# Attention with a one-expert MoE: p's four chunks packed 171 columns apart, and the second of its PSUM banks also lent out as a third single bank

## The chip, the cores and the metric

The kernel runs on one core of a Trainium2 chip. The metric is the device time of one execution in microseconds (us), as the median of the runs of the same program; lower is better.

## What is computed

The reference has two parts. The first is attention with pooled keys: `kv` (4 batches, 384 x 32 positions, 128 channels) is averaged over 4 x 4 patches to 768 positions and multiplied by `w_sr`, and the result serves as both keys and values for 12288 queries per batch:

```
s = scale * (q @ k.transpose(0, 2, 1))
a = np.exp(s - s.max(-1, keepdims=True))
a /= a.sum(-1, keepdims=True) + 1e-09
x = (a @ v).reshape(B * S, D)            # 49152 tokens, 128 channels
```

The second is a mixture of eight experts with one expert per token, the one whose gate logit is largest:

```
logits = x @ w_gate
e = argmax(logits);  gate = softmax(logits)[e]
y = gate * (np.maximum(x @ w1[e], 0.0) @ w2[e])
```

## The kernel before

**The blocks.** The 49152 tokens are cut into 96 blocks of 512 tokens (`block`, 24 per batch; a block is four chunks of 128 tokens). For a block, TensorE (PE) makes the scores in three pairs of banks (`scores`, tile `s`), ScalarE (ACT) takes `exp` of a pair (`e`, L897), VectorE (DVE) forms 1 + s - e in bf16 (`r`, L899), and PE multiplies the four chunks of `r` by the values (`values`, L914): nine matmuls for a chunk, 145 or 136 columns each, into the PSUM tile `po`. ACT and DVE take `po` apart into a high and a low fp16 part (`xp`, L929 and L930) and a copy of the logits (`lg`, L932), and a DMA turns `xp` into `x`. The expert part of an earlier block follows: `hidden` makes three tiles of hidden units (`ph`, one bank each, of three, one and one matmuls of 512 columns), ACT drains them (`X` L956, `g` L963), GpSimd (POOL) splits the first (`g` L958, L960), `rows` collects 32 matmuls of 128 columns in one bank (`py`), DVE scales it by the gate (`y`, L983) and a DMA writes it. In the page and in the rows each bank tile other than `s` and `po` is called `b`.

**PSUM.** `PSUM = {"s": 2, "po": 1, "b": 2}` (L320): two pairs of banks for `s`, one tile of two banks for `po` (chunks 256 columns apart, two to a bank), and two single banks `b`. The single banks serve the three hidden tiles and `py` of every block, and all small results of the preparation.

**The preparation.** While the blocks of one batch run, `keys` pools the next batch's `kv` and makes its keys, and `expert` prepares the expert that most tokens of the batch will take: norms, an order of hidden units, gathers of `w1` and `w2` by one-hot matrices (`PU`), all through the single banks. Near its end `po_` (another tile than `po`: a single bank) takes the product `pown`; `constant` (L831 to L837, four DVE instructions) reads it with a scale (`ws`, ready with `uy`) and adds a row to `w2U`. The op is given out as one piece and waits for `pown`, `uy`, `w2Ug` and `w2x`; the single bank of `po_` is held until it is done. After each of the first three batches, `general_step` handles tokens that belong to another expert: DVE finds them, POOL gathers their queries by an indirect DMA (L1212), and PE turns the gathered queries (L1231, tile `pq`) before the rest.

**What sets the order.** Nothing is issued in the order of the code. Each piece of work is an `Op` with an engine, an estimated duration, a due time and the tiles it needs; `Plan.order` (L105) simulates five engines and the slots of all pools with those estimates and always takes the op that can start first, by due time where several could. `Plan.issue` then writes the ops out in the order of their planned starts. In that list an op that takes a tile of a pool for the first time gets the slot that comes free first (L170), and the slot is taken until the last op that uses the tile has ended. The semaphores are put in afterwards by the tile framework, from the program's order and from what each instruction reads and writes. PE, ACT, DVE, POOL and the DMA queue of SP each work through their own list strictly in order, so an instruction that waits holds up all behind it. From 20 to 110 us the planner also fills gaps of PE with matmuls on constants (`fill`).

Of the kernel before, what the change touches and what calls it, by code (L numbers as in the profile page):

```python
# [9 lines left out]
F32 = mybir.dt.float32  # L10
# [51 lines left out]

TOKENS = {"qr", "qs", "qh", "qp", "qTh", "qT", "s", "e", "r", "po", "xh", "xl", "lg", "x", "ph", "gf", "gh", "g", "py", "ys", "o"}
NUDGE = {}


class Buf:
    def __init__(self, pool, make):
        self.pool, self.make, self.slot, self.tile, self.left, self.end = pool, make, None, None, 0, 0.0


class Op:
# [3 lines left out]
class Plan:  # L76
# [30 lines left out]
    def order(self):  # L107
# [15 lines left out]
        while count:  # L123
            best = None
            for e, ops in cand.items():
                pick = None
                for o in ops:
                    start = max(free[e], o.ready)
                    if o.lock:
                        start = max(start, locked)  # L130
                    for b in o.bufs:
                        if b.slot is None:
                            start = max(start, min(slots[b.pool]))
                    if start == math.inf:
                        continue
                    key = (max(start, free[e] + 0.1), o.at, o.n)
                    if pick is None or key < pick[0]:
                        pick = key, start, o
                if pick and (best is None or pick[1] < best[0]):
                    best = pick[1], pick[2]  # L140
# [26 lines left out]
            for b in o.bufs:  # L167
                first = b.slot is None
                if first:
                    b.slot = min(range(len(slots[b.pool])), key=lambda i: (slots[b.pool][i], i))  # L170
                    slots[b.pool][b.slot] = math.inf
                o.slot_of.append((b, first))
                b.left -= 1
                b.end = max(b.end, land)
                if not b.left:
                    slots[b.pool][b.slot] = b.end + 0.1
# [17 lines left out]
def attention_moe(ctx: ExitStack, tc, q, kv, w_sr, w_gate, w1, w2, out):  # L194
# [117 lines left out]
    def bc(t, n):  # L312
# [7 lines left out]
    PSUM = {"s": 2, "po": 1, "b": 2}  # L320
    plan = Plan({**SBUF, **PSUM})
    op = plan.op

    def buf(pool, shape, dtype=F32):
        where = psum if pool in PSUM else sb
        return Buf(pool, lambda name: where.tile(shape, dtype, name=name))

    def bank():
        return buf("b", [P, 512])
# [172 lines left out]
    def expert(b, at):  # L502
# [329 lines left out]
        def constant():  # L832
            t, sc = ow.tile, ws.tile[so, 15:16]
            nc.vector.tensor_scalar(t[so, 0], po_.tile[so, :P], sc, None, op0=ALU.mult)
            nc.vector.scalar_tensor_tensor(t[so, 1], po_.tile[so, :P], sc, t[so, 0], op0=ALU.mult, op1=ALU.subtract)
            nc.vector.tensor_scalar(t[so, 2], t[so, 0], own[so, UH:UH + 1], None, op0=ALU.mult)
            nc.vector.scalar_tensor_tensor(w2U.tile[so, UH - 1], t[so, 1], own[so, UH + 1:UH + 2], t[so, 2], op0=ALU.mult,  # L837
                                           op1=ALU.add)

        op("DVE", 1.0, constant, at + 31, [("pown", b), ("uy", b), ("w2Ug", b), ("w2x", b)], [("w2U", b)], [po_, ow, ws, w2U])  # L840
        op("DVE", .1, lambda: nc.vector.memset(cn[:, 31:32], 0.0), at + 36,
           [("Tb", b), ("uy", b), ("first", b), ("rest", b)], [("con", b)])

# [8 lines left out]
    def block(t):  # L852
# [30 lines left out]
               T - 1.4 * LEN, [("qp", t)], [("qTh", t), ("qT", t)], [qp, qT], lands=2.0, moves=1.2)  # L883

        r = buf("r", [P, KT, BLK], BF16)
        po = buf("po", [P, CH, 2 * P])
        for s in range(KT // 2):
            ps, e = buf("s", [P, 2, BLK]), buf("e", [P, 2, BLK])
            at = T + s * LEN / 3
# [16 lines left out]
        for c in range(CH):  # L906
            def values(c=c):
                for kt in range(KT):
                    mm(po.tile[:, c, :XW], r.tile[:, kt, c * P:(c + 1) * P], v16.tile[:, kt, :XW], kt == 0, kt == KT - 1)
                    if kt == 0:  # L910
                        for i, j in ((0, 0), (1, 0), (0, 1)):
                            mm(po.tile[:, c, :P + E], own_q(c, i), M.tile[:, j], False, False)

            op("PE", .55, values, T + LEN * (1.8 + c / 8), [("r", t), ("qT", t), ("Mx", b), ("v16x", b)], [("po", t, c), ("po", t)],  # L914
               [po, qT, r, M, v16])
        last = ("po", t)
        if t % NB == 0:
            k["lg"], k["mo"] = buf("lg", [P, NB * CH, XW - C]), buf("mo", [P, 4, NB * CH])
        if i == 0:
# [6 lines left out]
        xl = lambda: x.tile[:, CH:].rearrange("p j n -> p (j n)")  # L926
        xc = lambda c, i: x.tile[:, i * CH + c]
        A = T + LEN * 2.05
        op("ACT", .59, lambda: nc.scalar.copy(xp.tile[:, 0], po.tile[:, :, :C]), A, [last], [("xh", t)], [po, xp])  # L929
        op("DVE", .69, lambda: nc.vector.tensor_tensor(xp.tile[:, 1], po.tile[:, :, :C], xp.tile[:, 0], op=ALU.subtract),  # L930
           A + .5, [("xh", t)], [("xl", t)], [po, xp])
        op("ACT", .23, lambda: nc.scalar.copy(lg.tile[:, bs], po.tile[:, :, C:XW]), A + .6, [last], [("lg", t)], [po, lg])  # L932
        op("SP", 1.24, lambda: nc.sync.dma_start_transpose(x.tile, xp.tile.rearrange("p a j c -> p (a j c)")), A + 1,
           [("xl", t)], [("x", t)], [xp, x], lands=2.0, moves=1.2)
        if t == GROUPS[g][-1]:
# [5 lines left out]
        for u in range(UH):  # L941
# [20 lines left out]
            else:  # L962
                op("ACT", .69, lambda u=u, ph=ph, zu=zu: nc.scalar.activation(  # L963
                    gg.tile[:, u], ph.tile, AF.Relu, bias=zu()), at + .5,
                   [("ph", t, u), ("zb", b)], [("g", t)], [ph, gg, k["zb"]])
        py, y = bank(), buf("y", [P, CH, C])

        def rows():
            Lt, w = k["L"].tile, k["w2U"].tile
# [418 lines left out]
```

## Time and profile before

| | before |
|---|---|
| median of 3 runs | 855.87 us (855.49 to 857.4) |
| the profiled execution | 854.62 us, of which 852.9 us are the span from the first to the last instruction |
| PE busy | 774.7 us, 91% of the span |
| DVE busy | 657.8 us, 77% |
| ACT busy | 599.2 us, 70% |
| POOL busy | 577.1 us, 68% |
| chain that ended last | PE 53%, DVE 15%, POOL 10%, DMA 8%, ACT 8%, issue 4% |

"Busy" counts a matmul to its modelled end, so that a busy PE need not be a PE at its peak; a single matmul is some 0.17 us longer than the distance at which the next follows it. The "chain" follows the work that ended last back to the start, at each step to what released it. In the view of waits, a row names the engine and tile that waited, what it waited for, and the total, the number and the longest of these waits.

### The profile page before, as it was taken

The page shows a single profiled execution, that of the slowest core. Times are in us where ns is not written, and L with a number is a line of the kernel's source. Part 1 is how long each engine was busy: PE and PEld are TensorE (multiplying, and loading weights), DVE is VectorE, ACT ScalarE, POOL GpSimd, SP SyncE. Part 2 cuts the span into 40 slices and gives each one's busy share as a digit, 9 for nine tenths or more (in the row PEclk, how much of TensorE's full clock was granted, in tenths as well). Part 3 has the DMA queues.
Part 4 walks back from the last instruction along what each step waited for, and adds up shares of the span by engine and source line. Part 5 has one row for each costly group of instructions (what it writes and reads, how often), then busy time and mean ns, then how long its engine had stood idle before and what let it go on. Part 6 is the DMA issues. An engine that isn't in the chain of part 4 may idle for free.

```text
span 852.9 us, 22180 instructions
## 1 busy us (share of the span) xinstructions
PE 774.7 (91%) x8701; PEld 611.1 (72%) x8701; DVE 657.8 (77%) x1209; ACT 599.2 (70%) x958; POOL 577.1 (68%) x784
## 2 busy tenths in 40 slices
PE   5998899998999778999999987989999989999995
PEld 5586587786878656777776765777877867787774
DVE  4688777879779885867868998667897888767683
ACT  1466877877777556777678765677778776778772
POOL 0475889855689858656558997845657766657463
PEclk9999999999999999999999999999999999999998
DMA  9475989876788997776469879668466989656542
GB/s 334 120 187 107 224 190 242 170 148 119 144 207 194 200 187 195 161 133 152 103 144 226 216 166 251 145 146 181 88 122 147 162 173 191 135 118 130 117 102 64
DMA packets 328283, 139.48 MB, mean 164 GB/s; under 512 B 214590, under 2 KB 320194, under 8 KB 328176
## 3 DMA queue, kind: packets, MB, share of 16 engines
q1 hardware_dynamic: 327696, 137.80, 72.4%
q8 instruction: 69, 1.13, 0.6%
q14 instruction: 38, 0.31, 0.1%
q0 software_dynamic: 192, 0.17, 0.1%
q10 hardware_dynamic: 288, 0.07, 0.0%
HBM read 59.12 MB, written 26.94 MB: 101 GB/s over the span
## 4 chain that ended last, share of the span: by engine, by line
PE 53%; DVE 15%; POOL 10%; DMA 8%; ACT 8%; issue 4%; SPq 1%; POOLq 0%; ACTq 0%; DVEq 0%
PE b L306 26%; PE po L306 16%; PE s L306 10%; DVE r L899 6%; DMA kv<-in_kv_dram 2%; ACT e L897 2%; POOL g L960 2%; POOL kv L396 2%; DMA qT<-qp 2%; DMA gp<-in_q_dram,gi 2%; POOL qp L880 1%; DVE xp L930 1%; ACT g L963 1%; DMA x<-xp 1%; POOL g L958 1%
## 5 line engine op out<-in xcount | busy, mean ns | idle before, releaser
L899 DVE SCALAR_TENSOR_TENSOR r<-s,e 128x1024 bf16<-128x1024 f32 x288 | 347.6, 1216 | 88.7 <-ACT e L897 87.1
L897 ACT ACTIVATE e<-s 128x1024 f32<-128x1024 f32 x288 | 294.3, 1030 | 92.8 <-PE s L306 87.8
L306 PE MATMUL po<-v,r 128*128 128x145 f16 x2304 | 254.3, 230 | 8.2 <-DVE xp L930 6.3
L306 PE MATMUL s<-qT,KT 128*128 128x512 f16 x576 | 168.7, 380 | 23.2 <-DVE r L899 20.9
L306 PEld LDWEIGHTS <-r 128*128 128x128 bf16 x2304 | 171.0, 100 | 25.2 <-issue 4.6
L306 PE MATMUL b<-w2U,g 128*128 128x128 f16 x1920 | 171.7, 220 | 3.4 <-POOL g L960 3.2
L963 ACT ACTIVATE g<-b,zb 128x512 f16<-128x512 f32 x192 | 129.8, 691 | 37.1 <-PE b L306 36.5
L306 PE MATMUL b<-x,w1U 128*128 128x512 f16 x465 | 139.4, 379 | 10.9 <-ACT g L963 5.7
L306 PE MATMUL po<-M,qT 128*128 128x136 f16 x1152 | 133.2, 225 | 0.0
L306 PE MATMUL b<-L,x 128*128 128x128 f16 x1116 | 123.6, 220 | 6.7 <-ACT X L956 3.8
L306 PEld LDWEIGHTS <-g 128*128 128x128 f16 x1920 | 124.2, 98 | 4.3 <-POOL g L960 3.9
L960 POOL TENSOR_TENSOR g<-X,g 128x512 f16<-128x512 f32 x96 | 112.1, 1167 | 7.6
L880 POOL TENSOR_TENSOR qp<-qr,qp 128x512 f16<-128x512 f32 x94 | 110.9, 1180 | 5.8
L306 PEld LDWEIGHTS <-qT 128*128 128x128 f16 x1152 | 86.3, 99 | 38.4 <-issue 15.6
L876 POOL TENSOR_SCALAR qr<-qr,con 128x512 f32<-128x512 f32 x94 | 66.4, 707 | 55.1 <-DMA qr<-in_q_dram 54.9
L306 PEld LDWEIGHTS <-x 128*128 128x128 f16 x1116 | 81.3, 98 | 24.5 <-issue 12.8
L958 POOL CAST g<-X 128x512 f16<-128x512 f32 x96 | 60.0, 625 | 47.9 <-ACT X L956 47.4
L306 PEld LDWEIGHTS <-KT 128*128 128x128 bf16 x576 | 51.2, 99 | 57.1 <-issue 31.7
L930 DVE TENSOR_TENSOR xp<-po,xp 128x512 f16<-128x512 f32 x96 | 65.8, 685 | 27.3 <-ACT lg L932 15.9
L956 ACT ACTIVATE X<-b,zb 128x512 f32<-128x512 f32 x96 | 66.8, 695 | 24.5 <-PE b L306 23.8
L878 POOL CAST qp<-qr 128x512 f16<-128x512 f32 x94 | 59.4, 632 | 36.2 <-DMA qT<-qp 34.7
L983 DVE TENSOR_TENSOR y<-b,gt 128x512 f32<-128x512 f32 x96 | 65.1, 680 | 20.4 <-PE b L306 16.5
(346 smaller groups left out, 920.9 us busy)
## 6 DMA issues: line engine op xcount, KB each, us to landing
qr<-in_q_dram SPq DMA_DIRECT2D x96, 256.0 KB, 3.2
out_dram<-y SPq DMA_DIRECT2D x96, 256.0 KB, 2.7
kv<-in_kv_dram SPq DMA_DIRECT2D x41, 512.0 KB, 6.3
raw<-in_moe_w_dram SPq DMA_DIRECT2D x14, 512.0 KB, 5.0
e<-in_kv_dram SPq DMA_DIRECT2D x3, 512.0 KB, 8.6
v_dram<-vT SPq DMA_DIRECT2D x4, 384.0 KB, 3.3
qT<-qp SPq DMA_TRANSPOSE x94, 3.4
x<-xp SPq DMA_TRANSPOSE x93, 3.3
```

The costliest lines, as they stand in the source:

```text
L306: return nc.tensor.matmul(o, l, r, start=start, stop=stop)
L876: op("POOL", .71, lambda: nc.gpsimd.tensor_scalar(qr.tile, qr.tile, cn[:, 8:9], 1.0, op0=ALU.mult, op1=ALU.mult), T - 2 * LEN, [("qr", t), ...
L878: op("POOL", .63, lambda: nc.gpsimd.tensor_copy(qp.tile[:, 0], qr.tile), T - 1.9 * LEN, [("qs", t)], [("qh", t)], [qr, qp])
L880: op("POOL", 1.17, lambda: nc.gpsimd.tensor_sub(qp.tile[:, 1], qr.tile, qp.tile[:, 0]), T - 1.8 * LEN, [("qh", t)], [("qp", t)], [qr, qp])
L897: op("ACT", 1.03, lambda e=e, ps=ps: nc.scalar.activation(e.tile, ps.tile, AF.Exp), at + .6, [("s", t, s)], [("e", t, s)], [ps, e])
L899: op("DVE", 1.22, lambda e=e, ps=ps, s=s: nc.vector.scalar_tensor_tensor(r.tile[:, 2 * s:2 * s + 2], ps.tile, 1.0, e.tile, op0=ALU.add, op ...
L930: op("DVE", .69, lambda: nc.vector.tensor_tensor(xp.tile[:, 1], po.tile[:, :, :C], xp.tile[:, 0], op=ALU.subtract), A + .5, [("xh", t)], [ ...
L956: op("ACT", .69, lambda ph=ph, zu=zu: nc.scalar.activation(gf.tile, ph.tile, AF.Relu, bias=zu()), at + .5, [("ph", t, u), ("zb", b)], [("g ...
L958: op("POOL", .62, lambda: nc.gpsimd.tensor_copy(gg.tile[:, 0], gf.tile), at + 1.5, [("gf", t)], [("gh", t), ("g", t)], [gf, gg])
L960: op("POOL", 1.16, lambda: nc.gpsimd.tensor_sub(gg.tile[:, UH], gf.tile, gg.tile[:, 0]), at + 2, [("gf", t), ("gh", t)], [("g", t)], [gf, gg])
L963: op("ACT", .69, lambda u=u, ph=ph, zu=zu: nc.scalar.activation(gg.tile[:, u], ph.tile, AF.Relu, bias=zu()), at + .5, [("ph", t, u), ("zb" ...
L983: op("DVE", .69, lambda: nc.vector.tensor_tensor(y.tile, py.tile.rearrange("p (c d) -> p c d", d=C), bc(gr["gt"].tile[:, 0, js], C), op=AL ...
```

## The change

Three things change together.

First, the chunks of `po` stand 171 columns apart instead of 256. Chunks 0 to 2 then lie in the tile's first bank (columns 0 to 486 of its 512) and chunk 3 alone in the second (from column 513). The two banks become one tile `shared`, made once, which is never given out anew; `po` is a view of its first 684 columns.

Second, the tile's second bank is the third slot of the pool `b` (`"b": 3`). A block takes that slot (`po2`) with chunk 3 and gives it back after the last of the three reads of `po`. Any other user of `b` may have it in between, save `py`, which is kept to slots 0 and 1. `Buf.choose` picks the slot that is free first and makes the third one 0.6 us less attractive.

Third, `constant` becomes two ops: the two instructions that read `po_`, due at `at + 26` and waiting for `pown` and `uy` alone, and the other two (`constant2`), due at `at + 31` as before and locked into the sequence of locked ops.

```diff
+SPARE = 0.6
 class Buf:
-    def __init__(self, pool, make):
+    def __init__(self, pool, make, only=None):
+    def choose(self, slots, at):
+        s = slots[self.pool]
+        return min(self.only or range(len(s)), key=lambda i: (max(s[i], at) + SPARE * (self.pool == "b" and i == 2), s[i], i))
...
-                            start = max(start, min(slots[b.pool]))
+                            start = max(start, slots[b.pool][b.choose(slots, start)])
...
-                    b.slot = min(range(len(slots[b.pool])), key=lambda i: (slots[b.pool][i], i))
+                    b.slot = b.choose(slots, start)
...
-    PSUM = {"s": 2, "po": 1, "b": 2}
+    PSUM = {"s": 2, "po": 1, "b": 3}
+    PO = 171
+    shared = psum.tile([P, 2, 512], F32, name="po0")
...
+        views = {"po0": lambda: shared.rearrange("p b x -> p (b x)")[:, :CH * PO].rearrange("p (c x) -> p c x", x=PO),
+                 "b2": lambda: shared[:, 1]}
+        return Buf(pool, lambda name: views[name]() if name in views else where.tile(shape, dtype, name=name), only)
...
             nc.vector.tensor_scalar(t[so, 0], po_.tile[so, :P], sc, None, op0=ALU.mult)
             nc.vector.scalar_tensor_tensor(t[so, 1], po_.tile[so, :P], sc, t[so, 0], op0=ALU.mult, op1=ALU.subtract)
+        def constant2():
+            t = ow.tile
             nc.vector.tensor_scalar(t[so, 2], t[so, 0], own[so, UH:UH + 1], None, op0=ALU.mult)
...
-        op("DVE", 1.0, constant, at + 31, [("pown", b), ("uy", b), ("w2Ug", b), ("w2x", b)], [("w2U", b)], [po_, ow, ws, w2U])
+        op("DVE", .5, constant, at + 26, [("pown", b), ("uy", b)], [("own2", b)], [po_, ow, ws])
+        op("DVE", .6, constant2, at + 31, [("own2", b), ("w2Ug", b), ("w2x", b)], [("w2U", b)], [ow, w2U], lock=True)
...
-        po = buf("po", [P, CH, 2 * P])
+        po, po2 = buf("po", None), buf("b", None, only=(2,))
...
-               [po, qT, r, M, v16])
+               [po, qT, r, M, v16] + [po2] * (c == CH - 1))
...
-        py, y = bank(), buf("y", [P, CH, C])
+        py, y = buf("b", [P, 512], only=(0, 1)), buf("y", [P, CH, C])
```

The reads of `po` (L929, L930, L932 of before) hold `po2` beside `po`. Since all places come from the planner's simulation, the order changes on every engine. Three places show how.

**PE, within a block of the third batch** (tiles with their numbers, and the engines whose semaphores an instruction waits for). `x,w1U` is a hidden tile's matmul, `v,r` and `M,qT` are those of a chunk of `po`, `KT` is a score. Before, the end of a `py`, one hidden tile in bank `b0` and the start of a later chunk:

```order
L306 MATMUL b1_7101<-w2U1_3393,g1_7053 128x128
L306 LDWEIGHTS w1U1_3331
L306 MATMUL b0_7142<-x2_6294,w1U1_3331 128x512 [waits Activation_49]
L306 LDWEIGHTS r1_6893
L306 MATMUL po0_7079<-v161_2446,r1_6893 128x145
L306 LDWEIGHTS qT1_6764
L306 MATMUL po0_7079<-M1_2658,qT1_6764 128x136
```

With the change, a hidden tile in the third slot, which the names now call `po0_145` like the chunks; chunk 0 follows it, then a hidden tile in `b0`, chunk 1 (both left out but for their first rows), a score pair and chunk 2:

```order
L313 LDWEIGHTS w1U1_3223
L313 MATMUL po0_145<-x2_6224,w1U1_3223 128x512 [waits DVE_49]
L313 LDWEIGHTS r2_6780
L313 MATMUL po0_145<-v161_2378,r2_6780 128x145
...
L313 MATMUL b0_6995<-x2_6224,w1U1_3223 128x512 [waits Activation_49]
...
L313 LDWEIGHTS KT1_2422 [waits DMAHW5_49]
L313 MATMUL s0_7008<-qT2_6921,KT1_2422 128x512 [waits DVE_49]
...
L313 MATMUL po0_145<-v161_2378,r2_6780 128x145 [waits Activation_49]
```

The hidden tiles now stand between the chunks of `po`, and a chunk in the middle of a block carries a wait for ACT, which it did not before.

**DVE, end of the second batch's expert.** Before, with the last three of a block's `r`, the bias `zb` and the four instructions of `constant`:

```order
L899 SCALAR_TENSOR_TENSOR r_3432<-s_3387,e_3405 128x1024
L822 TENSOR_REDUCE zb_3449<-b_3407 128x3
L823 SCALAR_TENSOR_TENSOR zb_3449<-zb_3449,own 128x3
L834 TENSOR_SCALAR own_3458<-b_3098,ws_2889 2x128
L835 SCALAR_TENSOR_TENSOR own_3458<-b_3098,ws_2889,own_3458 2x128
L836 TENSOR_SCALAR own_3458<-own_3458,own 2x128
L837 SCALAR_TENSOR_TENSOR w2U_3393<-own_3458,own 2x128
```

With the change:

```order
L845 TENSOR_SCALAR own_3193<-b_3070,ws_2864 2x128
L846 SCALAR_TENSOR_TENSOR own_3193<-b_3070,ws_2864,own_3193 2x128
L914 SCALAR_TENSOR_TENSOR r_3083<-s_3089,e_3108 128x1024
...
L945 TENSOR_TENSOR xp_3248<-po_145,xp_3248 128x512
L1020 RECIPROCAL gt_3280<-gt_3280 128x16
L833 TENSOR_REDUCE zb_3320<-b_3250 128x3
L834 SCALAR_TENSOR_TENSOR zb_3320<-zb_3320,own 128x3
L850 TENSOR_SCALAR own_3193<-own_3193,own 2x128
L851 SCALAR_TENSOR_TENSOR w2U_3277<-own_3193,own 2x128
```

The two reads of the bank now stand six rows ahead of the bias, with `r` and `xp` of the blocks between; the other two stay behind the bias.

**ACT, in the first `general_step`,** down to the copy of the turned queries (`pool`). Before:

```order
L956 ACTIVATE X0_5189<-b1_5172,zb1_3449 128x512
L897 ACTIVATE e0_5194<-s1_5186 128x1024
L963 ACTIVATE g0_5198<-b1_5196,zb1_3449 128x512
L963 ACTIVATE g0_5198<-b0_5205,zb1_3449 128x512
L932 COPY lg1_3949<-po0_5113 128x68
L956 ACTIVATE X1_5228<-b1_5210,zb1_3449 128x512
L1227 COPY gk1_5269<-s0_5221 128x768
L897 ACTIVATE e2_5282<-s1_5274 128x1024
L897 ACTIVATE e1_5300<-s0_5279 128x1024
L963 ACTIVATE g1_5271<-b0_5287,zb1_3449 128x512
L1232 COPY pool1_5335<-b1_5285 128x128
```

With the change:

```order
L971 ACTIVATE X0_5095<-po0_145,zb1_3320 128x512
L912 ACTIVATE e1_5114<-s1_5100 128x1024
L978 ACTIVATE g0_5118<-b1_5116,zb1_3320 128x512
L978 ACTIVATE g0_5118<-po0_145,zb1_3320 128x512
L912 ACTIVATE e0_5152<-s0_5141 128x1024
L944 CAST xp1_5204<-po0_145 128x512
L947 COPY lg1_3945<-po0_145 128x68
L971 ACTIVATE X1_5207<-b1_5145,zb1_3320 128x512
L1242 COPY gk1_5240<-s1_5213 128x768
L978 ACTIVATE g1_5222<-b1_5226,zb1_3320 128x512
L912 ACTIVATE e2_5263<-s0_5244 128x1024
L912 ACTIVATE e1_5277<-s1_5248 128x1024
L1247 COPY pool1_5291<-b0_5252 128x128
```

One `e` and one `xp` more stand between the first hidden tile and the turned queries, and two of the hidden tiles are read from the third slot.

## Rows read from the trace of the kernel before

**Rows 1.** The page: busy time by engine; the chain that ended last.
```profile
PE 774.7 (91%) x8701; PEld 611.1 (72%) x8701; DVE 657.8 (77%) x1209; ACT 599.2 (70%) x958; POOL 577.1 (68%) x784
PE 53%; DVE 15%; POOL 10%; DMA 8%; ACT 8%; issue 4%; SPq 1%; POOLq 0%; ACTq 0%; DVEq 0%
```

**Rows 2.** Windows: start:end, length, busy by engine (instructions), PE clock, DMA, GB/s.
```profile
200.00:270.00 70.00, 67.33 (x823) 53.18 (x823) 56.82 (x83) 52.60 (x86) 53.59 (x73) 1.00 0.77 166
270.00:340.00 70.00, 57.24 (x632) 44.63 (x630) 53.76 (x106) 43.24 (x70) 55.41 (x62) 0.95 0.91 203
480.00:550.00 70.00, 59.49 (x635) 45.51 (x634) 56.82 (x111) 45.76 (x74) 59.98 (x70) 0.95 0.86 204
```

**Rows 3.** Waits of PE, whole span: waiter <- releaser, us in total, times, longest.
```profile
PE s L306 <- DVE r L899: 21.1, 31, 2.7
PE b L306 <- ACT g L963: 9.3, 16, 1.5
PE b L306 <- ACT X L956: 7.2, 9, 1.7
PE po L306 <- DVE xp L930: 6.3, 9, 1.3
PE b L1231 <- DMA gp<-in_q_dram,gi: 5.3, 2, 3.2
PE b L415 <- ACT X L956: 0.8, 2, 0.4
PE b L306 <- DVE y L983: 0.7, 2, 0.4
```

**Rows 4.** Timeline, two single banks used twice: start, us, engine, instruction [idle <-releaser].
```profile
278.99 1.06 ACT L897 ACTIVATE e<-s 128x1024 f32<-128x1024 f32 x1
...
280.67 0.33 PE L306 MATMUL b<-L,x 128*128 128x128 f16 x3 [1.72 <-ACT X L956]
...
412.02 0.81 PE L306 MATMUL b<-x,w1U 128*128 128x512 f16 x3
...
412.83 0.59 PE L306 MATMUL s<-qT,KT 128*128 128x512 f16 x2
...
413.05 0.70 ACT L956 ACTIVATE X<-b,zb 128x512 f32<-128x512 f32 x1
...
413.80 0.38 PE L306 MATMUL b<-x,w1U 128*128 128x512 f16 x1 [0.38 <-ACT X L956]
```

**Rows 5.** Timeline, weight loads of one chunk of p.
```profile
408.04 0.41 PEld L306 LDWEIGHTS <-r 128*128 128x128 bf16 x6
```

**Rows 6.** Timeline, the gathers of the first two general steps.
```profile
319.52 1.27 POOL L1212 DMA_INDIRECT gp<-in_q_dram,gi  x1 [0.17 <-issue]
...
326.27 0.14 PEld L1231 LDWEIGHTS b<-ident,gp 128*128 128x128 f32 x1 [3.68 <-DMA gp<-in_q_dram,gi]
...
532.83 0.41 PE L1231 MATMUL b<-ident,gp 128*128 128x128 f32 x1 [2.12 <-DMA gp<-in_q_dram,gi]
```

**Rows 7.** Windows in which the bank of po_ is held (four), and stretches after them.
```profile
58.90:84.20 25.30, 22.16 (x218) 16.19 (x217) 21.77 (x46) 18.24 (x31) 16.14 (x22) 0.93 0.68 113
197.20:219.10 21.90, 18.94 (x225) 14.71 (x224) 19.47 (x37) 15.21 (x27) 11.73 (x20) 1.00 0.66 123
410.70:426.70 16.00, 14.69 (x169) 11.03 (x167) 13.57 (x23) 11.82 (x19) 8.58 (x15) 1.00 0.50 111
616.80:636.40 19.60, 18.34 (x216) 14.07 (x216) 17.79 (x34) 14.49 (x25) 9.36 (x18) 1.00 0.68 124
219.10:241.00 21.90, 21.90 (x285) 17.77 (x283) 16.23 (x21) 16.44 (x25) 15.11 (x18) 1.00 0.87 208
426.70:442.70 16.00, 15.55 (x179) 11.56 (x177) 9.66 (x13) 12.94 (x20) 9.30 (x12) 1.00 0.58 130
636.40:656.00 19.60, 19.60 (x245) 15.41 (x243) 14.10 (x19) 15.59 (x24) 13.92 (x19) 1.00 0.74 153
```

**Rows 8.** Groups by line and shape: instruction, count, busy us, mean ns, idle before.
```profile
L306 PE MATMUL b<-slots 128*128 128x384 f16 x78 | 14.8, 325 | 0.2
```

More of the change, by code (lines that the diff above doesn't have):

```diff
@@ L64 @@
 NUDGE = {}
+SPARE = 0.6
 class Buf:
-    def __init__(self, pool, make):
-        self.pool, self.make, self.slot, self.tile, self.left, self.end = pool, make, None, None, 0, 0.0
+    def __init__(self, pool, make, only=None):
+        self.pool, self.make, self.only, self.slot, self.tile, self.left, self.end = pool, make, only, None, None, 0, 0.0
+    def choose(self, slots, at):
+        s = slots[self.pool]
+        return min(self.only or range(len(s)), key=lambda i: (max(s[i], at) + SPARE * (self.pool == "b" and i == 2), s[i], i))
 class Op:
@@ L319, in attention_moe, with buf @@
             "lp": 2, "gs": 1, "gi": 1, "le": 1, "gg": 1, "gk": 2, "gp": 1}
-    PSUM = {"s": 2, "po": 1, "b": 2}
+    PSUM = {"s": 2, "po": 1, "b": 3}
+    PO = 171
+    shared = psum.tile([P, 2, 512], F32, name="po0")
     plan = Plan({**SBUF, **PSUM})
     op = plan.op
-    def buf(pool, shape, dtype=F32):
+    def buf(pool, shape, dtype=F32, only=None):
         where = psum if pool in PSUM else sb
-        return Buf(pool, lambda name: where.tile(shape, dtype, name=name))
+        views = {"po0": lambda: shared.rearrange("p b x -> p (b x)")[:, :CH * PO].rearrange("p (c x) -> p c x", x=PO),
+                 "b2": lambda: shared[:, 1]}
+        return Buf(pool, lambda name: views[name]() if name in views else where.tile(shape, dtype, name=name), only)
     def bank():
@@ L928, in block @@
         A = T + LEN * 2.05
-        op("ACT", .59, lambda: nc.scalar.copy(xp.tile[:, 0], po.tile[:, :, :C]), A, [last], [("xh", t)], [po, xp])
+        op("ACT", .59, lambda: nc.scalar.copy(xp.tile[:, 0], po.tile[:, :, :C]), A, [last], [("xh", t)], [po, po2, xp])
         op("DVE", .69, lambda: nc.vector.tensor_tensor(xp.tile[:, 1], po.tile[:, :, :C], xp.tile[:, 0], op=ALU.subtract),
-           A + .5, [("xh", t)], [("xl", t)], [po, xp])
-        op("ACT", .23, lambda: nc.scalar.copy(lg.tile[:, bs], po.tile[:, :, C:XW]), A + .6, [last], [("lg", t)], [po, lg])
+           A + .5, [("xh", t)], [("xl", t)], [po, po2, xp])
+        op("ACT", .23, lambda: nc.scalar.copy(lg.tile[:, bs], po.tile[:, :, C:XW]), A + .6, [last], [("lg", t)], [po, po2, lg])
         op("SP", 1.24, lambda: nc.sync.dma_start_transpose(x.tile, xp.tile.rearrange("p a j c -> p (a j c)")), A + 1,
```

## The prediction

> **What bounds the kernel now.** I read the page first, then the windows, the waits of PE, and the timeline at the places that these name. PE is busy 91% of the span and makes 53% of the chain that ended last; DVE has 15%, POOL 10%, ACT and DMA 8% each [rows 1]. So PE's list is what the time follows, and the question is where PE stands still. The windows show that this differs by stretch: from 200 to 270 us PE is idle for 2.7 us of 70, from 270 to 340 for 12.8 and from 480 to 550 for 10.5, and there the granted clock falls to 0.95 in the mean [rows 2]. The last two are the stretches of the first two general steps. The waits tell on what PE stands [rows 3]: 21.1 us on a pair of score banks (`r` must have been read out), 6.3 us on `po`, and on single banks 9.3 + 7.2 + 0.8 (ACT draining a hidden tile) + 0.7 (DVE's `y`). That makes **18.0 us of waits on single banks**, the sum that a third slot can address. 5.3 us are waits for the gathered queries.
>
> **What a wait on a bank costs.** The timeline shows one bank used twice [rows 4]: the matmuls of a hidden tile end at 412.83, ACT drains it from 413.05 for 0.70 us, and the next hidden tile in that bank starts at 413.80, 0.97 us after the first ended. A score pair stood in between, so that only 0.38 us was idle. I take 1.0 us less the PE work in between as the price of such a place; the longest wait of the kind, 1.72 us at 280.67, is one where ACT had an `e` of 1.06 us first. PE's work is counted with the distances of the rows: six weight loads in 0.41 us are 62 ns apart [rows 5], so a chunk of `po` (nine matmuls) is 0.56 us; a score pair is some 0.43 us (0.59 with its tail) and a hidden tile of one matmul 0.22 us.
>
> **Term 1, the third slot.** In the order before, 87 users of a single bank come with less than 1.0 us of PE work behind the last matmul of the bank's former user; what is missing to 1.0 us adds up to 29 us, of which the trace shows 18.0 as waits (0.62). In the new order these are about 54, missing 21 us. So the third slot takes away 8 us of shortfall, or 8 x 0.62 = 5.0 us. Bounds: nothing (each wait taken away is followed by the wait for a score pair, 21.1 us of which stay), and 18.0 us, if no wait on a bank were left.
>
> **Term 2, the waits that the shared tile adds.** `po` and the third slot are now one tile, `shared`, and the semaphores come from the tile framework, not from the planner. The order with its waits shows what that does: a chunk in the middle of a block waits for ACT, though it writes the tile's first bank and ACT read the second. Before, only the first chunk of a block ever waited. Following the counts of the semaphores through the built program: ACT and DVE read the third slot 69 times with a wait for PE, and 50 of these wait not for the matmul that filled it but for a later chunk of `po`, whichever was issued last; with slots 0 and 1 nearly every read waits for its own matmul. And 33 times chunks 0 to 2 wait for such a read (chunk 3, which really needs the bank, 22 times). So chunk, drain and chunk run one after another where the planner laid them side by side. Where the next chunk follows with 0 to 0.64 us of PE work between, the price above leaves 0.4 to 1.0 us. Over all chunks the shortfall is 21 us (16 on chunks 0 to 2, 5 on chunk 3 through the late drains), of which 1.5 us are in term 1 already; the same share of 0.62 gives 19.5 x 0.62 = **12.1 us**. Bounds: zero, if PE reaches these chunks late anyhow, and 21 us and more where ACT has an `e` of 1.03 us ahead.
>
> The 50 late drains also hold ACT for up to one chunk, 50 x 0.56 = 28 us. ACT is busy 70% of the span [rows 1], and what is queued behind the drain is mostly the next `e`, for which DVE's `r` and then PE wait. I take 1 us for this, with bounds of 0 and 8 us.
>
> **Term 3, the general steps.** The gather starts at 319.52 and PE stands at 326.27 until it has landed; in the second step PE waits 2.12 us at 532.83 [rows 6]. The new order puts more work of PE between the matmul that finds the rows and the turned queries: about 9.3 us instead of 6.4, a chunk and score pair among it (the piece of ACT's order shows their `e` and `xp`). That 2.9 us covers most of 3.2 and all of 2.1 us. I take 4 us of the 5.3, since the work must itself be ready there. Bounds 0 and 5.3.
>
> **Term 4, the split of `constant`.** The bank of `po_` is held from the product to the second read, 25.3, 21.9, 16.0 and 19.6 us in the four experts, and PE is idle 3.1, 3.0, 1.3 and 1.3 us in these windows, 8.7 us of 82.8. In the stretches behind three of them it is idle 0, 0.45 and 0 us [rows 7]. One bank for all else is one reason; the other is DVE, busy 13.6 to 21.8 us of these windows with the same expert's work, which stays. The waits on banks in them are in term 1; of the rest I take 1 us. Bounds 0 and 7. The four instructions are the same and the two that follow the bias get shorter as an op; no queue is lengthened.
>
> **At nothing:** the reads of `po` move the same elements; the planner's filling of gaps in the start grows by five times three matmuls on constants, at 325 ns each with their tails [rows 8], laid into time in which PE waits for `kv`. Without that cover it would be 2.5 us. The clock could gain or lose with PE's gaps in the two stretches at 0.95; I take zero.
>
> **Sum:** -5.0 + 12.1 + 1 - 4 - 1 = +3.1 us on the profiled execution of 854.62 us, or 857.7. That execution lies 1.25 us under the median of 855.87, which makes **859.0 us**, 0.4% slower.
>
> **The rivals.**
> *Faster: the new waits are covered.* If the chunks that wait for a drain come late anyhow, or PE's stop only takes the place of a wait for a score pair (21.1 us are there to be absorbed), terms 1, 3 and 4 stand alone: -10.0 us, so 845.9. Half of the cover gives 852. For it speaks that 47% of the chain is not PE's; against it that there are stretches such as 219 to 241 us in which PE never stands [rows 7], where each stop counts in full. The waits on banks are what rows 3 show. The Trainium skill (Perfetto Trace Analysis, Matmul Optimizations) says that all eight banks of PSUM should be used; by that rule the idle second bank of `po` is a plain loss and the time would be that of this rival. The trace of before agrees with the rule as far as rows 3 go.
> *No change.* Terms cancel within 1.7 us: it needs term 2 at about 9 us, somewhat under half of its shortfall. Here belongs also that the change does not do what it says: of 288 hidden tiles the new order puts only 51 into the third slot, since `po` itself holds it for a good part of each block. Then 855.9.
> *Much slower: the odd columns.* Chunks 1 and 3 start at columns 171 and 513, odd ones; every chunk of before starts at an even one, so no row shows the difference. These are 18 matmuls a block, 1728 in all, 62 ns apart [rows 5], 107 us. The mechanism decides the sign from about 4% more per matmul (4 us); with 10% the time is 870. The Trainium skill (Advanced Engine Details and Errata, PSUM Cachelines) gives lines of two fp32 values and asks that consecutive pairs be contiguous; a run of 145 columns is contiguous at either start, so that it bears on the first and last column at most, and no run here shows it yet.
>
> **How the numbers follow.** Slower by the shared tile: 0.48, with a range of its own from 857.6 to 870. Faster: 0.31. No change: 0.17. Odd columns: 0.04. About 0.2%, 1.7 us, is what a measurement of this kernel can tell from no change. So faster 0.31, same 0.17, slower 0.52. The range must reach to the faster rival, since this holds more than 0.2: from 846 us, its full size, to 870 us, where term 2 stands at its full 21 us, the late drains at 5 and the gains at half.
>
> **What would show it.** Waits of PE on `po` released by ACT's `X` and `g` in the middle of a block, some 10 to 17 us in all (term 2); ACT's `X` and `g` with a tile named `po` as their input starting behind a chunk and not behind their own matmul. Waits of PE on `b` for ACT down from 17.3 to some 12 us (term 1). The two waits for the gather gone or under 1 us (term 3). PE idle below 8.7 us in windows of the same work (term 4). Chunks with 62 ns between matmuls at all four places rule out the odd columns. The prediction is wrong if the waits on `po` stay at the 8 us of before while those on `b` fall, or if the waits on score pairs fall by as much as those on `po` grow.

## The result, and the profile after

The changed kernel takes 865.7 us (median), the kernel before 855.7: the ratio is 1.0116, with a 95% interval from 1.0074 to 1.0158. The change makes the kernel about 10 us slower, in the direction of the forecast and within its range, but 6.7 us above its centre of 859.0: the loss is three times the 3.1 us that were forecast. One hundredth of the time is 8.6 us; ratios below are turned into microseconds by that. Each ratio is of a kernel's fast runs to those of the kernel before made beside them (medians 854.7 to 855.7 us), so it is not exactly the quotient of the medians given.

First come the two rows of the page that answer to [rows 1].

```profile
PE 781.2 (90%) x8716; PEld 612.4 (71%) x8716; DVE 659.4 (76%) x1209; ACT 600.4 (70%) x958; POOL 576.3 (67%) x784
PE 62%; DVE 10%; ACT 10%; DMA 7%; POOL 6%; issue 4%; SPq 0%; ACTq 0%; POOLq 0%; DVEq 0%
```

The work is the same but for the planner's 15 matmuls on constants; the chain now runs through PE for 62% of the span instead of 53%, and DVE's share of it fell from 15% to 10%. PE thus waits less for `r`, and stands elsewhere. The waits of PE say where. They answer to [rows 3]; the columns are total, number and longest.

```profile
PE s L313 <- DVE r L914: 11.9, 18, 2.0
PE b L313 <- ACT g L978: 10.1, 10, 2.0
PE po L313 <- ACT g L978: 9.7, 20, 1.1
PE po L313 <- DVE xp L945: 4.2, 5, 1.3
PE b L1246 <- DVE r L914: 4.1, 2, 2.1
PE b L313 <- ACT X L971: 4.0, 8, 1.3
PE po L313 <- ACT X L971: 2.5, 5, 0.8
PE b L313 <- DVE y L998: 1.0, 2, 0.5
```

Waits for a score pair fell from 21.1 to 11.9 us, those for single banks from 18.0 to 15.3 (10.1, 4.0, 1.0 and 0.2 on another line). New are the rows in which PE waits on `po` for ACT's `g` and `X`, 12.2 us; three smaller rows of the kind, for `gp`, `pT` and `Ms`, add 2.9. Before there was no such row. The groups by line tell the same from the side of the chunks. Here is the idle time ahead of the matmuls of `r` by `v` (count, busy us, mean ns, idle and what ended it), after and, below, before.

```profile
L313 PE MATMUL po<-v,r 128*128 128x145 f16 x2304 | 257.0, 229 | 17.2 <-ACT g L978 9.1 <-DVE xp L945 3.2 <-ACT X L971 1.7
```

```profile
L306 PE MATMUL po<-v,r 128*128 128x145 f16 x2304 | 254.3, 230 | 8.2 <-DVE xp L930 6.3 <-ACT lg L932 1.9
```

Before, chunks stood for 8.2 us, always at the first chunk of a block, for the reads of the last one. Sorted by the place of the chunk in its block (worked out from the trace, waits over 0.1 us), the changed kernel has 4.4 us on chunk 0, 9.6 us in 20 waits on chunks 1 and 2, which share no bank with the third slot, and 3.0 us in 8 waits on chunk 3, which does: 12.6 us within a block.

The timeline shows one such stop whole (start, us, engine, instruction, idle before it and its releaser).

```profile
816.73 0.81 PE L313 MATMUL po<-x,w1U 128*128 128x512 f16 x3
...
817.37 0.23 PE L313 MATMUL po<-v,r 128*128 128x145 f16 x1
...
818.17 0.48 PE L313 MATMUL po<-v,r 128*128 128x145 f16 x5
818.74 0.69 ACT L971 ACTIVATE X<-po,zb 128x512 f32<-128x512 f32 x1 [0.37 <-issue]
...
819.48 0.22 PE L313 MATMUL po<-v,r 128*128 128x145 f16 x1 [0.82 <-ACT X L971]
```

The first two chunks of a block end at 818.65. ACT's `X` reads a hidden tile in the third slot, whose matmuls (816.73) were issued ahead of these chunks, but starts only behind them, at 818.74, after 0.37 us in which ACT stood idle; chunk 2, which lies in the other bank, waits for this read, 0.82 us, and starts at 819.48. Chunk, drain, chunk, as the prediction had it.

**Where the time is lost.** Counting PE's work back from the end (each matmul counted by its columns, four times if it is fp32; this is a way of counting, the same for all kernels) gives the time at which both kernels have the same work left. The changed kernel is 8.0 us ahead when 160 us of work are left (675 us into the span before), 1.2 us behind at 120 (720 us), 1.9 behind at 60 (777 us) and 12.7 behind at 20 (819 us). So the batches with a preparation gain, the stretch around the third general step gives that back, and the last blocks, with no preparation beside them, add the rest. The windows show both sides: the first two general steps as in [rows 2], then a stretch of the last blocks.

```profile
270.00:340.00 70.00, 61.76 (x661) 47.21 (x662) 55.27 (x94) 47.81 (x76) 58.38 (x68) 0.95 0.90 208
480.00:550.00 70.00, 62.88 (x706) 47.79 (x703) 56.22 (x104) 50.45 (x84) 60.59 (x72) 1.00 0.96 219
795.00:830.00 35.00, 31.53 (x362) 24.15 (x360) 22.60 (x29) 23.18 (x37) 16.94 (x24) 0.95 0.59 114
```

The same last stretch before:

```profile
795.00:830.00 35.00, 34.06 (x429) 26.98 (x427) 26.39 (x44) 27.58 (x44) 18.25 (x34) 1.00 0.46 107
```

PE's idle time fell from 12.8 to 8.2 us and from 10.5 to 7.1 us in the first two windows, but rose from 0.9 to 3.5 us of 35 in the last, where the granted clock is 0.95 instead of 1.00 in the mean.

### The profile page after: what moved, and what is told of

It reads as the page before. It is cut to its first block, busy times and chain, and to the rows that moved or that the text cites. A ratio compares the mean times of both kernels' runs of the same rounds, so it can differ in the third digit from the quotient of the medians.

```text
span 863.7 us, 22278 instructions
## 1 busy us (share of the span) xinstructions
PE 781.2 (90%) x8716; PEld 612.4 (71%) x8716; DVE 659.4 (76%) x1209; ACT 600.4 (70%) x958; POOL 576.3 (67%) x784
## 4 chain that ended last, share of the span: by engine, by line
PE 62%; DVE 10%; ACT 10%; DMA 7%; POOL 6%; issue 4%; SPq 0%; ACTq 0%; POOLq 0%; DVEq 0%
PE b L313 29%; PE po L313 21%; PE s L313 11%; DMA qT<-qp 5%; ACT e L912 4%; DVE r L914 4%; ACT g L978 3%; DMA kv<-in_kv_dram 2%; POOL kv L407 2%; POOL g L975 1%; DVE xp L945 1%; ACT X L971 1%; POOL qp L895 1%; POOL g L973 1%; ACT xp L944 1%
## 5 line engine op out<-in xcount | busy, mean ns | idle before, releaser
L313 PE MATMUL po<-v,r 128*128 128x145 f16 x2304 | 257.0, 229 | 17.2 <-ACT g L978 9.1
L313 PE MATMUL s<-qT,KT 128*128 128x512 f16 x576 | 168.3, 381 | 17.5 <-DVE r L914 11.9
L313 PE MATMUL b<-x,w1U 128*128 128x512 f16 x404 | 124.1, 382 | 6.9 <-ACT g L978 3.8
L978 ACT ACTIVATE g<-b,zb 128x512 f16<-128x512 f32 x147 | 98.8, 692 | 21.8 <-PE b L313 21.6
L313 PEld LDWEIGHTS <-x 128*128 128x128 f16 x1116 | 81.5, 99 | 21.0 <-issue 11.5
L998 DVE TENSOR_TENSOR y<-b,gt 128x512 f32<-128x512 f32 x96 | 64.8, 677 | 15.9 <-PE b L313 14.8
L971 ACT ACTIVATE X<-b,zb 128x512 f32<-128x512 f32 x90 | 62.5, 694 | 19.3 <-PE b L313 18.6
```

Source lines behind the costliest of these rows:

```text
L313: return nc.tensor.matmul(o, l, r, start=start, stop=stop)
L971: op("ACT", .69, lambda ph=ph, zu=zu: nc.scalar.activation(gf.tile, ph.tile, AF.Relu, bias=zu()), at + .5, [("ph", t, u), ("zb", b)], [("g ...
L998: op("DVE", .69, lambda: nc.vector.tensor_tensor(y.tile, py.tile.rearrange("p (c d) -> p c d", d=C), bc(gr["gt"].tile[:, 0, js], C), op=AL ...
```

## The experiments

Theory A says that the loss is the false waits through the shared tile. Theory B says that a third slot, or the order that it brings, is a loss by itself. Theory C says that odd columns cost time. All ratios are to the kernel before, with 95% intervals.

### The columns alone

The kernel before, in its own order, with `po` packed:

```diff
-        po = buf("po", [P, CH, 2 * P])
+        po = Buf("po", lambda name: psum.tile([P, 2, 512], F32, name=name).rearrange("p b x -> p (b x)")[:, :CH * 171].rearrange("p (c x) -> p c x", x=171))
```

> The kernel before, in its own order on every engine, but with the chunks of po 171 columns apart (three in the first bank, one in the second, starts 0, 171, 342 and 513); the third slot is not lent. Theory A and B: 855.7, within 1.5 us. Theory C (a start at an odd column, or three chunks in one bank, costs time): 859 or more, with the matmuls of chunks 1 and 3 more than 62 ns apart.

Measured: 0.9993 (0.9971 to 1.0015). The weight loads of a chunk stand at the distance of [rows 5], six in 0.41 us:

```profile
406.33 0.41 PEld L306 LDWEIGHTS <-r 128*128 128x128 bf16 x6
```

The mean matmul of `r` by `v` takes 230 ns as before. Theory C is out: neither an odd start nor three chunks in one bank costs anything that can be told here (0.15 hundredths, 1.3 us, at the upper end of the interval). The sentence of the Trainium skill (Advanced Engine Details and Errata, PSUM Cachelines) that consecutive pairs should be contiguous is not touched by this: 145 contiguous columns did as well from an odd start as from an even one.

### The same order with and without the shared tile

The three reads of `po` cover both banks. If each is cut into one instruction for chunks 0 to 2 and one for chunk 3, the two banks can be tiles of their own, and the semaphores then follow the banks. The planner's durations stay, so that the order of instructions is the same on all engines (the traces of the control and of the two tiles have the same sequence on PE, ACT, DVE and POOL). The control cuts the reads but keeps the shared tile; a second control cuts the reads of the kernel before.

```diff
-        op("ACT", .59, lambda: nc.scalar.copy(xp.tile[:, 0], po.tile[:, :, :C]), ...)
+        def high():
+            nc.scalar.copy(xp.tile[:, 0, :3], po.tile[:, :3, :C])
+            nc.scalar.copy(xp.tile[:, 0, 3], po.tile[:, 3][:, :C])
...
+        op("ACT", .59, high, ...)
```

and for the two tiles, on top of it:

```diff
-    shared = psum.tile([P, 2, 512], F32, name="po0")
...
+        views = {"po0": lambda: psum.tile([P, 512], F32, name="po0")[:, :510].rearrange("p (c x) -> p c x", x=170)}
...
-        po, po2 = buf("po", None), buf("b", None, only=(2,))
+        po, po2 = buf("po", None), buf("b", [P, 512], only=(2,))
...
+                to = po.tile[:, c] if c < CH - 1 else po2.tile
...
-            nc.scalar.copy(xp.tile[:, 0, 3], po.tile[:, 3][:, :C])
+            nc.scalar.copy(xp.tile[:, 0, 3], po2.tile[:, :C])
```

The control, with the shared tile:

> The changed kernel with each of the three reads of po (xp high, xp low, lg) cut into one instruction for chunks 0 to 2 and one for chunk 3; order, columns and shared tile as in the changed kernel. It is the control for the run with two tiles. All theories: two more instructions of ACT and one of DVE per block, so slower than the changed kernel's 865.7 us by 2 to 8 us: 868 to 874. The waits of PE on po released by ACT's X, g, pT, Ms and gp stay near the 15 us of the changed kernel.

The two tiles:

> As the run with the reads in two, and in the same order of instructions on every engine, but chunks 0 to 2 lie in a tile of their own and chunk 3 in a tile of the third slot (chunks 170 columns apart), so that semaphores only join instructions which touch the same bank. Theory A (the loss is the waits through the shared tile): the 15 us of waits on po released by ACT's X, g, pT, Ms and gp fall to the true ones, some 3 us, and the time is 8 to 15 us under the run with the reads in two. Theory B (the loss is the new order itself, which PE cannot follow as planned): within 2 us of the run with the reads in two. Theory C (odd columns): chunk 1 and the start of chunk 3 are now even; the distance between the matmuls of these chunks would fall below 62 ns.

The kernel before with its reads cut:

> The kernel before, with the reads of po cut in two as in the run above; order unchanged. It prices the additional instructions by themselves: 96 x 3 instructions, 2 to 8 us over 855.7, so 858 to 864. If the price is the same as the difference between the run with the reads in two and the changed kernel, it can be taken off the run with two tiles.

Measured: the control 871.9 us, 1.0161 (1.0104 to 1.0218); the two tiles 853.9 us, **1.0006** (0.9972 to 1.0039); the kernel before with cut reads 857.6 us, 1.0041 (1.0017 to 1.0066). In the same order of instructions the shared tile costs 1.0161 - 1.0006 = 1.55 hundredths, 13 us, give or take 6 by the two intervals (the medians alone would give 18). The rows of waits, first of the control:

```profile
PE po L313 <- ACT g L990: 9.7, 20, 1.1
PE po L313 <- DVE xp L950: 5.2, 7, 1.2
PE po L313 <- ACT X L983: 2.5, 5, 0.8
```

and of the two tiles, all that is left on `po`:

```profile
PE po L313 <- DVE xp L948: 2.7, 4, 1.1
PE po L313 <- ACT lg L953: 0.7, 1, 0.7
```

Chunks 1 and 2 no longer wait at all. Theory A holds for this part of the loss. But 1.0006 is not a gain: with the price of the cut reads (0.0041, 3.5 us) taken off, the third slot and the split together bring only 3 us (give or take 4), where the prediction's terms 1, 3 and 4 summed to 10.

### The third slot for whole blocks

The other way to be rid of the stops inside a block is to let the planner know: a block takes the third slot with its first chunk, so that nothing stands between its chunks in the shared tile.

```diff
-               [po, qT, r, M, v16] + [po2] * (c == CH - 1))
+               [po, qT, r, M, v16] + [po2])
```

> The changed kernel, but a block takes the third slot with its first chunk instead of its fourth, so no hidden tile can stand in the shared tile between two chunks of one block; the planner lays out its order by that. Theory A (waits through the shared tile): the waits on po released by ACT in the middle of a block vanish (under 3 us), the waits on single banks rise a little, since the slot is lent less often; 849 to 856 us. Theory B (a third slot in the order is a loss by itself): 860 us or more.

Measured: 855.5 us, 0.999 (0.9959 to 1.002). All waits of chunks are on chunk 0 (12.8 us, of which 3.7 are still for ACT's `g`, which reads the tile's other bank; here the planner has counted them). By the count of work left, this kernel is 12.8 us ahead of the one before at 160 us of work and still 9.1 at 60, and then loses 12.7 us until 20 are left. Without any false wait in the middle of a block the last blocks are a loss here too, which neither theory had.

### The last 16 blocks with two single banks

```diff
-            ph = bank()
+            ph = buf("b", [P, 512], only=(0, 1) if t >= 80 else None)
```

This keeps the hidden tiles of blocks 80 to 95 out of the third slot; the blocks before have it as they had. It was done to the changed kernel, to the one with whole blocks and to the one with two tiles.

> The changed kernel, but the hidden tiles of the last 16 blocks (t of 80 and more) are kept to the two single banks. The changed kernel loses 11.6 us against the kernel before over the last 80 us of PE's work. Theory A (waits through the shared tile, 7.5 us of them on po in that stretch): 854 to 859. Rival (the loss there is not the third slot's): 863 or more.

> The kernel in which a block takes the third slot with its first chunk, and the hidden tiles of the last 16 blocks (t of 80 and more) are kept to the two single banks. The run without the second part is 10 us ahead of the kernel before when 60 us of PE's work are left, and loses 13 us from there. Theory A (it loses them through the third slot in these blocks, by waits between hidden tiles and chunks): the lead stays, 844 to 849. Rival (the end of the program is bound by something that a lead can't move, such as the DMAs of the last blocks): 853 to 857.

> The run with two tiles (reads of po in two), and the hidden tiles of the last 16 blocks kept to the two single banks. The run with two tiles still loses 5 us against the kernel before over the last 60 us of PE's work. Theory A (in those blocks a third slot that po also needs is a loss even where all waits are true ones): 847 to 850. Rival (the loss in those blocks is the shared tile's false waits alone): 853 to 856, as the run with two tiles.

Measured: the changed kernel 853.9 us, 0.9977 (0.9946 to 1.0008); whole blocks **843.5 us, 0.9854** (0.9794 to 0.9914); two tiles 847.1 us, 0.989 (0.986 to 0.9921). Taking the third slot from the last 16 blocks is worth 1.39, 1.36 and 1.16 hundredths, some 12, 12 and 10 us, each give or take 4 to 6. The order of PE's work is the same up to these blocks in each pair. In the stretch between 60 and 20 us of PE's work before the end, PE's pauses of over 0.2 us between two matmuls add up to

| kernel | pauses, us |
|---|---|
| before | 0.8 |
| changed | 10.0 |
| reads in two, shared tile | 9.8 |
| reads in two, two tiles | 5.2 |
| whole block | 13.2 |
| changed, last 16 blocks with two banks | 1.0 |
| two tiles, last 16 blocks with two banks | 0.8 |
| whole block, last 16 blocks with two banks | 1.2 |

(worked out from the matmuls' starts and their columns). About half of the changed kernel's pauses there stay with two tiles. Two of its eight pauses, 2.3 us by this count, are true waits at the hand-over of the third slot, one in each direction:

```profile
809.83 0.38 PE L313 MATMUL b<-x,w1U 128*128 128x512 f16 x1
810.40 0.69 ACT L989 ACTIVATE g<-b,zb 128x512 f16<-128x512 f32 x1
...
811.14 0.22 PE L313 MATMUL b<-v,r 128*128 128x145 f16 x1 [0.94 <-ACT g L989]
...
813.15 0.28 DVE L949 TENSOR_TENSOR xp<-b,xp 128x128 f16<-128x128 f32 x1
...
813.48 0.81 PE L313 MATMUL b<-x,w1U 128*128 128x512 f16 x3 [1.07 <-DVE xp L949]
```

Chunk 3 (`b<-v,r`) waits 0.94 us until ACT has drained the hidden tile that stood in its bank; the next hidden tile waits 1.07 us until DVE has read chunk 3 out. Two single banks in turn do not have this, since `po` takes no part in them. The other six, 2.9 us, are waits for score pairs, for `y` and for drains of hidden tiles. The pairs of runs thus show what the third slot costs in these blocks; that it costs it by the hand-overs is seen for 2.3 us alone, and the two profiled executions with two tiles differ by 5.0 us in all. Why the same hand-overs cost less in the batches before is argued only: there the preparation gives PE other work.

The whole-block version beats both kernels. Its page, in the rows of [rows 1]:

```profile
PE 774.0 (92%) x8716; PEld 608.3 (72%) x8716; DVE 662.3 (79%) x1209; ACT 600.3 (71%) x958; POOL 572.3 (68%) x784
PE 60%; DVE 13%; DMA 8%; POOL 7%; ACT 7%; issue 4%; SPq 0%; ACTq 0%; POOLq 0%; DVEq 0%
```

### The split by itself, and without it

> The kernel before with nothing but the end of the expert's preparation in two ops (own2 at +26, constant2 at +31, locked); two single banks, chunks 256 columns apart. The prediction's term 4 gave 1 us with bounds of 0 and 7: 848.7 to 855.7, taken 854.7. A rival: the loss of the changed kernel comes from the split's order (the lock): then 860 or more.

> The changed kernel with the end of the preparation as one op again. If the split is worth 1 to 4 us by itself, 866 to 870. If the split is what made the changed kernel slower, 850 to 857.

> The run with two tiles (chunks 0 to 2 and chunk 3 in tiles of their own, reads of po in two), but the end of the preparation as one op again. Theory A (the shared tile's waits are the loss in any order): 13 to 18 us under the 870.8 us of the changed kernel without the split, plus some 3 for the reads in two: 856 to 861. Rival (the third slot is a loss without the split, whatever the tile): 866 or more. Against the run with two tiles and the split (853.9) it prices the split where a third slot is there: 0 to 1.5 us if it is worth the same as on the kernel before, about 5 us if it is worth what the changed kernel shows.

> The fastest kernel so far (the third slot taken with a block's first chunk, two single banks for the hidden tiles of the last 16 blocks; 843.5), with the end of the preparation as one op again. Where the split is worth what the pairs with a third slot show (5 to 6 us): 848 to 850. Where it is worth what it shows on the kernel before (0 to 1.5 us): 843 to 845.

Measured: the split alone on the kernel before 855.9 us, 0.9982 (0.9946 to 1.0019), no difference that can be told, as term 4 had it. The changed kernel without the split 870.8 us, 1.0205 (1.0177 to 1.0233); with two tiles and no split 860.3 us, 1.0051 (1.0015 to 1.0087); the fastest kernel without the split **874.1 us, 1.0237** (1.0186 to 1.0288). So the same split is worth 1.5 us with two slots (give or take 3), 8 and 4 us in the changed order with the shared and with two tiles (each give or take 4), and 33 us (give or take 7) where a block needs the third slot from its first chunk. Neither expectation of the last run had that. Its trace shows where most of it begins. Here are PE's instructions on the shared tile, and DVE's reads of `po_`, in the second expert.

```profile
200.51 0.48 PE L313 MATMUL po<-v,r 128*128 128x145 f16 x5
203.72 0.49 PE L313 MATMUL po<-Ms,cbc 128*128 128x128 f32 x2
```

```profile
217.62 0.36 DVE L845 TENSOR_SCALAR own<-po,ws 2x128 f16<-2x128 f32 x1
218.02 0.36 DVE L846 SCALAR_TENSOR_TENSOR own<-po,ws,own 2x128 f16<-2x128 f32 x1
```

```profile
219.88 0.23 PE L313 MATMUL po<-v,r 128*128 128x145 f16 x1
```

`po_` (`po<-Ms,cbc`) has been given the third slot, and DVE makes its second read only with the last pieces of the preparation, 14.3 us later. Until then no chunk can start: PE has no chunk for 16.2 us from the product on, and for 15.9 and 16.3 us in the third and fourth experts. By the count of work left, the kernel falls behind the one with the split by some 8, 6 and 7 us in these stops and the 20 to 50 us that follow each, about 20 of the 31 us between the two profiled executions; the rest has not been traced to a place. With the split the second read of the same bank comes after 3.7 us:

```profile
199.02 0.49 PE L313 MATMUL po<-Ms,cbc 128*128 128x128 f32 x2
...
202.71 0.36 DVE L846 SCALAR_TENSOR_TENSOR own<-po,ws,own 2x128 f16<-2x128 f32 x1
203.12 0.22 PE L313 MATMUL po<-v,r 128*128 128x145 f16 x1 [0.19 <-DVE own L846]
```

Of the changed kernel without the split the trace shows a milder form: `po_` in the third slot in three experts, each with 13.6 us between two chunks. The rival for the pair with two tiles, that the third slot is a loss without the split whatever the tile, falls with 860.3 us: the shared tile's part there is 1.0205 - 1.0051 = 1.54 hundredths, and 3.5 us more with the cut reads taken off: 13 to 17 us, give or take 4.

## Why the prediction was right, and where it was not

**Term 2, the false waits, was right in kind and size.** Forecast: 12.1 us, and 1 us for late drains. Waits of PE on `po` for ACT in the middle of a block: 10 to 17 us were forecast, 12.6 came, 9.6 on chunks 1 and 2 and 3.0 on chunk 3, where 62% of 16 and of 5 us had been taken; with the other users of the slot, such as hidden tiles, it is 15.1. Taking the shared tile away in the same order gave 13 us (6 either way). What the 1 us for late drains was in truth has not been measured apart.

**Terms 1, 3 and 4 together were mis-sized for one reason: term 1 was bounded by zero from below.** The prediction let a third slot bring nothing or a gain, since "each wait taken away is followed by the wait for a score pair". It did not ask what a slot costs that `po` itself must have back in every block. In the last 16 blocks that costs some 10 us, give or take 4, even with two tiles. Elsewhere the gains were if anything larger than forecast: the two-tile kernel with its last blocks on two banks stands at 0.989, which with the cut reads taken off is -1.5 hundredths or -13 us, against -10 forecast. The shared tile is worth 13 us by the pair above and 11 by the pair with its last blocks on two banks (0.9977 and 0.0041 for the cut reads, against 0.989). So the account of the changed kernel is about -13, +10 for the last blocks and +11 to +13 for the shared tile, +8 to +10 in all, where +9.9 was measured, and not -10 and +13.

**The direction is in part luck.** With the gains and the false waits as they were measured, the prediction's own terms come to -13 + 11 to 13, or about nothing. The changed kernel with its last 16 blocks on two single banks, which is the test of that, stands at 0.9977 (0.9946 to 1.0008). Slower came true by the loss in the last blocks, which no term had.

**The upper end of the range was added up wrongly.** With term 2 at 21 us, the late drains at 5 and the gains at half, the time is 855.9 + 21 + 5 - 5 = 877 us and not 870.

**Inside these terms the routes were other ones.** Waits on single banks fell by 2.7 us only (forecast 5.0); those on score pairs fell by 9.2, which no term had. The prediction had named a fall of that kind as a sign that it was wrong: they fell by 9.2 us while the waits on `po` grew by about 13, so by these sums most of one may have been paid by the other, as the rival of covered waits had it; no run takes the two apart. Term 3 expected the waits at the gathers to be gone or under 1 us; they are 2.08 and 1.97 us, 4.1 of 5.3. The row names DVE's `r` for them, but PE starts 0.1 us behind the landing of each gather, at 321.62 and 525.90 us. The two stretches did gain, 8.0 us by their windows, of which 1.2 us by that wait.

**Term 4 was right in size for the kernel before; the windows of the changed one say little.** The bank of `po_` is held 9.4, 8.4, 9.9 and 9.9 us instead of 25.1, 21.6, 15.7 and 19.3 up to DVE's second read. The windows from the product to the end of the expert's preparation are now:

```profile
57.90:84.20 26.30, 23.55 (x237) 17.74 (x236) 24.34 (x48) 18.40 (x31) 18.28 (x25) 0.94 0.67 120
198.20:212.60 14.40, 11.97 (x157) 9.62 (x156) 12.57 (x29) 8.37 (x16) 6.63 (x12) 1.00 0.45 100
404.10:420.20 16.10, 15.13 (x183) 11.66 (x181) 14.90 (x31) 11.77 (x21) 7.75 (x13) 1.00 0.65 116
607.50:623.60 16.10, 15.13 (x183) 11.64 (x181) 14.65 (x31) 11.75 (x21) 7.93 (x13) 1.00 0.56 129
```

In them PE is idle for 2.8, 2.4, 1.0 and 1.0 us, 7.1 in all against the 8.7 of [rows 7]. But they are shorter, 72.9 us instead of 82.8, and the idle share hardly fell, from 10.5% to 9.8%. The split alone gave 1.5 us (give or take 3) where 1 was taken. What the prediction missed is that the split is worth far more once `po_` can land in a slot that chunks need.

**The rivals.** The odd columns are ruled out. The faster rival, 845.9 us, asked for the new waits to be covered; in the changed kernel they are not, but where the order avoids them within a block and the last blocks keep two banks, 843.5 us was measured. The rule on which it stood, of the Trainium skill (Perfetto Trace Analysis, Matmul Optimizations), to use all eight banks of PSUM, goes with the 0.9854 of the bank lent between blocks and withheld at the end, and not with the 1.0116 of the bank lent as in the change: here the sign was decided by who else needs the bank, and when.

**What stays open.** Around the third general step (from 160 to 120 us of work left) the changed kernel gives back 9 us of lead; the split alone, the two no-split versions of the changed order and both versions with two tiles give back 4 to 9 us there as well (worked out in the same way), the whole-block versions only 2 to 4. Here is this stretch in the changed kernel:

```profile
665.00:720.30 55.30, 45.78 (x519) 35.33 (x517) 44.91 (x98) 37.26 (x57) 31.83 (x49) 0.96 0.79 158
```

and before:

```profile
673.00:718.90 45.90, 42.43 (x518) 33.05 (x515) 38.92 (x91) 34.27 (x53) 30.36 (x46) 1.00 0.92 182
```

PE's pauses of over 0.2 us add up to 11.5 us against 4.5 before (9.6 with the split alone, 7.8 in the fastest kernel). The three longest of the changed kernel, 2.1 to 2.2 us each, are on single banks and a score pair, not on the shared tile. The granted clock adds to it: it stood at its lower level, 1.2 instead of 2.4 GHz, for 3.4 us from 678.0 and from 719.0 us, each time soon after PE had stood still for 2.0 us (a third stop as long, which ended at 699.6 us, had no such fall behind it); in the kernel before it stood at its upper level throughout this stretch. The share missing, 0.04 of 55 us, is some 2 us, an estimate. No run was made to tell why the pauses come. Nor was it tried to tell the planner of the false waits in another way than by whole blocks.

## What to carry to other kernels

When a buffer is lent out in the gaps of its main user, price the hand-over in both directions, in the stretch where nothing else is there to fill it; a new slot in a planner can be worth less than nothing. When two users come to share one tile, count what the framework will order by tile and not by bytes: here about half of what was lost (11 to 13 of 21 to 23 us) was waits between instructions that touch different banks, and following the semaphores through the built program gave their size before any run. An edit's worth depends on the order that stands around it: the same split was worth nothing that can be told on the kernel before, and 33 us on the fastest one.

## What the runs showed of the hardware

Cutting a read of PSUM in two cost little on the engines that read it: the ACT cast of 512 columns (0.59 us) became casts of 384 and 128 columns of 0.48 and 0.28 us, which overlap in part. On the kernel before, 192 additional ACT instructions raised ACT's busy time from 599.2 to 609.4 us, 96 of DVE raised that of DVE from 657.8 to 662.6, and the time rose by 3.5 us (0.0041, 0.0017 to 0.0066). Matmuls of 145 columns took 232 and 229 ns in the mean in chunks 1 and 3 with an odd start, and 232 and 227 ns in the same chunks with an even one.
